# A packed-attention and gated-MLP kernel on one core: its stages rewritten as generators, five conversion adds moved from VectorE to GpSimd, one load of 97 rows made one of 128

## The chip, the cores and the metric

The kernel runs on 1 core of one Trainium2 chip. The metric is the device time of one execution in microseconds (us). The kernel before takes 637.4 us, the median of three runs (636.73 to 638.5).

The engines are named as the profile names them: PE (TensorE's matmuls) and PEld (its weight loads), DVE (VectorE), ACT (ScalarE), POOL (GpSimd), SP (SyncE, which issues every DMA here). Each engine works through its own list of instructions in order.

## What is computed

Three blocks follow each other, for 8 batches of 576 positions and 512 channels.

```
# 1. attention through 32 packed queries per head (8 heads of 64)
p_packed = softmax(p @ k.T / 8) @ v
x = softmax(q @ p_packed.T / 8) @ p_packed
# 2. gated block: causal convolution of 5 taps, w_val and w_out are 512 x 512
gate_pre = sum_k conv_w[k] * xp[:, k:k + S]
x = (sigmoid(gate_pre) * (x @ w_val)) @ w_out
# 3. spatial block: w_in 512 x 1024, w_spatial 576 x 576, w_out2 512 x 512
h = relu(x @ w_in);  u, v = h[..., :512], h[..., 512:]
v_n = (v - mean(v)) / sqrt(var(v) + 1e-6)
v_s = w_spatial @ v_n + b_spatial
out = (u * v_s) @ w_out2
```

The weights of blocks 2 and 3 (except `w_spatial`) arrive as 64-bit floats and are turned into 32-bit ones on the chip.

## The kernel before

**Tiling.** Channels lie on the partitions, in 4 chunks of 128. The 576 positions are taken in two halves of 288, or in row blocks of 128, 128, 128, 128 and 64 (`KT`). Most products are made in three matmuls from a high and a low part of each factor; `split` (L89) makes the parts, the high one with a copy on ACT (L90), the low one with a subtraction on DVE (L91). All products run through `mms` (L93; its matmuls are L95).

**Weights.** `load_raw` (L484) loads 64-bit rows. `from_f64` (L456) turns a 128x512 piece into floats with five instructions in a row: an ACT activation into `tmp` (L460), two integer TENSOR_SCALARs on DVE (L464, L467), one SCALAR_TENSOR_TENSOR on DVE (L468), which writes the destination, and an add (L471), whose engine is an argument, `last`. `unit` (L490) gives `nc.vector` there for the five pieces named in `DADD` (L19) and `nc.gpsimd` for the others. Pieces are `woT` (w_out), `winv` and `winu` (the two halves of w_in) and `wval`; their tokens are `uo`, `uw`, `uu` and `uv`. The temporaries of `uo`, `uw` and `uv` come from four buffers, that of `uu` from one (`late`, L482), so that each `uu` waits for the add of the one ahead.

`fold` (L499, tokens `fv`, `fu`) multiplies w_out by w_in once, so that blocks 2 and 3 share one matrix, `wp`: 4 matmuls of plain 32-bit floats, each of which the profile shows as two instructions, then an ACT copy (L506) and a DVE subtraction (L507).

**Spatial weights.** `spatial` (L509, tokens `ws0` to `ws4`) loads 128 rows of the transposed spatial matrix into a buffer `stage` (L514) and splits them. The fifth, `ws4`, loads the last 64 rows, stored twice, as 128 rows (L517), and then 97 rows more, which hold them again and the bias (L520). From these it makes a copy of 32 rows (L522) and splits rows 0 to 63 and row 96 through a tile `hi` (L90, L91).

**Order of the work.** Three tables list stages by token: `START` (weights, and the first batch's attention), `FIRST` (the first batch's MLP, with the second batch's attention and the rest of the weights in between) and `LOOP` (the same for each further batch, without weights). `run` (L559) calls the stage of each token. The instructions so recorded are then set in order for each engine by a scheduler with a priority in the order of recording; a tile has to find a free buffer of its pool.

**The stages around the change.** `sa` (L136) makes the scores of the packed queries and their exponents, `tr` (L170) transposes them, `av` (L175) multiplies them by v; for the first batch `av` also multiplies by the convolution's taps into `ppk` (L197). `sb` and `sb2` make the second softmax (its normalisation is L239, its transpose L243), `cx` (L283) makes the first batch's gates, `val` (L323) the values times the gates, and `hv` (L349) the normalised rows `vn`: matmuls, a relu on ACT (L364), statistics on DVE (L371 to L375), one power on POOL (L376), and a TENSOR_SCALAR on DVE (L377). The pool `ps2` has four PSUM buffers, which all products share.

Of the kernel before, what the change touches and what calls it, by code (L numbers as in the profile page):

```python
# [16 lines left out]
P = 128  # L17
UGB = 5
DADD = ('u2', 'o0', 'o1', 'w1', 'w0')  # L19
START = """  # L20
ik0 ip0 ro0 ic0 ik1 sa0 iv1 uo0 iv0 rw0 tr0 lv0 rv0 ro1 uo1 cw0 rv1 cb0 lk0 lq0 rw1 uw0 tr1 uo3 uw1 av0 uw2 uo2 uv0 av1 uv1 uw3 lq1 fv3 fv0 fv1 lk1 ppt0 sb0 sb20 sb21 fv2 uv3 uv2 lp0 m0 cx0 cx1 lv1
"""
FIRST = """
val1 ru1 val0 val3 ru0 lv0 val2 sa0 uu2 uu0 hv0 uu1 tr0 ws3 tr1 uu3 fu2 fu0 ws4 hv3 wo0 lv1 ws1 hv2 av0 av1 fu1 lq0 fu3 ppt0 lq1 wo1 hv1 hv4 ws0 sb0 hu1 hu2 ws2 sb20 lp0 hu3 sb21 hu0 wo3 lk0 lk1 sp0 sp2 sp1 wo2 sp3 m0 xt0 out1 xt1 out3 out0 out2
# [7 lines left out]
def packed_attention_gated_mlp(  # L32
# [72 lines left out]
    def load_kq(kind, b, g):  # L105
        src = kT if kind == "k" else qT
        t = kq_p.tile([P, 2, S], F32, tag="kq", name="kq")
        nc.sync.dma_start(out=t, in_=src[b, g])
        kq_t[kind, b, g] = t

    def load_v(b, g):
        t = v_p.tile([P, 4, 5, 65], F32, tag="v", name="v")
        nc.sync.dma_start(out=t, in_=vT[b, g])
        v_t[b, g] = t

    def load_p(b):
        t = sm_p.tile([P, NC * NPK], F32, tag="pbd", name="pbd")
        nc.sync.dma_start(out=t, in_=pT[b])
        pbd_t[b] = t

    class Attn:
        def __init__(self, b):
            self.b = b
            self.a, self.aT = {}, {}
            self.sT, self.A, self.an = {}, {}, {}
            self.gate = {}

# [8 lines left out]
        def sa(self, _):  # L136
            ps, heads = self.heads(pbd_t.pop(self.b), "k")
            for i in range(0, 8, 2):
                for qt in range(4):
                    for g, h, pT_, k in heads[i:i + 2]:  # L140
# [4 lines left out]
                        )  # L145
            mx = sm_p.tile([P, 8], F32, tag="mx", name="mx")
# [13 lines left out]
            for g in range(2):  # L160
                a = f_p.tile([P, S], F32, tag="f", name="a")
# [8 lines left out]
        def tr(self, g):  # L170
            aT = sm_p.tile([P, NB, NPK], F32, tag="aT", name="aT")
            nc.vector.transpose(out=aT.rearrange("p a b -> p (a b)"), in_=self.a.pop(g))
            self.aT[g] = aT

        def av(self, g):  # L175
# [12 lines left out]
            if g == 0:  # L188
# [3 lines left out]
            nc.vector.reciprocal(rs, rs)  # L192
            nc.scalar.activation(out=self.pp[:, g, :], in_=ps[:, :64], func=AF.Copy, scale=rs)
            if self.b == 0:
                if g == 0:
# [6 lines left out]
        def ppt(self, _):  # L202
            ps = ps2.tile([P, 2, 512], F32, tag="ps2", name="ps2")[:, 0, :P]
            nc.tensor.transpose(ps, self.pp.rearrange("p a b -> p (a b)"), ident)
            self.ppT = pp_p.tile([P, P], F32, tag="ppT", name="ppT")
            nc.scalar.copy(out=self.ppT, in_=ps)

        def sb(self, _):
# [8 lines left out]
            for g in range(2):  # L217
                self.softmax_n(g, ps[g])

        def softmax_n(self, g, ps):  # L220
# [8 lines left out]
            )  # L229
            nc.scalar.activation(out=sTf, in_=sTf, func=AF.Exp, scale=scale)  # L230
            self.sT[g] = sT

        def sb2(self, g):
# [9 lines left out]
            nc.vector.transpose(out=an, in_=sT.rearrange("p a b -> p (a b)"))  # L243
            hi = am_p.tile([P, S], F32R, tag="Ah", name="Ah")
            lo = am_p.tile([P, S], F32R, tag="Al", name="Al")
            split(hi, lo, an)
            self.A[g] = (hi, lo)
            self.an[g] = an

        def m(self, _):  # L250
            ps = ps2.tile([P, 2, 512], F32, tag="ps2", name="ps2")
            for h in range(4):
                hs = slice(NPK * h, NPK * h + NPK)
                for g in range(2):
# [4 lines left out]
                    )  # L259
            hi = am_p.tile([P, 2, DM], F32R, tag="Mh", name="Mh", bufs=1)  # L260
            lo = am_p.tile([P, 2, DM], F32R, tag="Ml", name="Ml", bufs=1)
            split(hi, lo, ps)
            self.M = (hi, lo)

        def xt(self, n):
# [9 lines left out]
            if n == 0:  # L275
# [3 lines left out]
            if n == 1:  # L279
                for c in range(4):  # L280
                    self.conv(c, self.x[c // 2][:, c % 2, :])

        def cx(self, n):  # L283
            ps = [ps2.tile([P, 2, 512], F32, tag="ps2", name="ps2") for _ in range(2)]
            for tap in reversed(range(CONV)):
                sft = CONV - 1 - tap
                lo = sft if n == 0 else 0
                for h in range(4):
                    hs = slice(NPK * h, NPK * h + NPK)
                    for g in range(2):  # L290
# [4 lines left out]
                        )  # L295
            for c in range(4):
                if n == 0:
# [5 lines left out]
        def conv(self, c, x):  # L303
            gt = ug_p.tile([P, S], F32, tag="ug", name="gate")
            self.gate[c] = gt
            acc = f_p.tile([P, S], F32, tag="f", name="acc")
            nc.scalar.activation(out=acc, in_=x, func=AF.Copy, scale=cw[:, c, CONV - 1:CONV])  # L307
            for tap in range(CONV - 1):
# [4 lines left out]
                )  # L313
            nc.scalar.activation(out=gt, in_=acc, func=AF.Sigmoid)

    class Mlp:
        def __init__(self, at):
# [3 lines left out]
            self.vn = None  # L321

        def val(self, c):  # L323
# [3 lines left out]
            for n in range(2):  # L327
# [7 lines left out]
                )  # L335
            t = f_p.tile([P, S], F32, tag="f", name="g1")
            nc.vector.tensor_tensor(  # L337
                out=halves(t), in0=ps[:, :, :SH], in1=halves(at.gate.pop(c)), op=ALU.mult
            )
            g = g_p.tile([P, 2, S], F32R, tag="g", name="g")  # L340
            split(g[:, 0, :], g[:, 1, :], t)
            if not self.g1:
# [4 lines left out]
            self.g1[c] = g  # L347

        def hv(self, tt):  # L349
# [11 lines left out]
            vr = vr_p.tile([P, DM], F32, tag="vr", name="vr")  # L361
            if w == P:
                mm3(ps, [((g1[k][:, 0, ts_], g1[k][:, 1, ts_]), (w_hi[k], w_lo[k])) for k in range(NC)])
                nc.scalar.activation(out=vr, in_=ps, func=AF.Relu)  # L364
            else:
                mms(ps, [(self.tail[:, k, :], wk) for k in range(NC) for wk in (w_hi[k], w_lo[k])])
                nc.scalar.copy(out=vr[:w], in_=ps[w:])
                nc.vector.tensor_tensor(out=vr[:w], in0=ps[:w], in1=vr[:w], op=ALU.add)
                nc.scalar.activation(out=vr[:w], in_=vr[:w], func=AF.Relu)
            st = sm_p.tile([P, 6], F32, tag="st", name="st")  # L370
# [16 lines left out]
        def hu(self, c):
            ps = ps2.tile([P, 2, 512], F32, tag="ps2", name="ps2")
            cs = slice(P * c, P * c + P)
            for n in range(2):  # L390
# [10 lines left out]
                )  # L401
            u = ug_p.tile([P, S], F32, tag="ug", name="u")
            nc.scalar.activation(out=halves(u), in_=ps[:, :, :SH], func=AF.Relu)
            self.u[c] = u

        def sp(self, c):
            ps = ps2.tile([P, 2, 512], F32, tag="ps2", name="ps2")
            cs = slice(P * c, P * c + P)
            for n in range(2):
# [12 lines left out]
                )  # L422
            t = f_p.tile([P, S], F32, tag="f", name="g2")
            nc.vector.tensor_tensor(  # L424
                out=halves(t), in0=ps[:, :, :SH], in1=halves(self.u.pop(c)), op=ALU.mult
            )
            g = g_p.tile([P, 2, S], F32R, tag="g", name="g")
            split(g[:, 0, :], g[:, 1, :], t)
            self.g2[c] = g

        def out(self, e):
            ps = ps2.tile([P, 2, 512], F32, tag="ps2", name="ps2")
            cs = slice(P * e, P * e + P)
            for n in range(2):
# [10 lines left out]
                )  # L445
            t = f_p.tile([P, S], F32, tag="f", name="o")
            nc.scalar.copy(out=halves(t), in_=ps[:, :, :SH])  # L447
            nc.sync.dma_start(out=outT[self.b, e], in_=t)
# [7 lines left out]
    def from_f64(dst, raw, n, pool, tag, last=nc.gpsimd):  # L456
# [5 lines left out]
        )  # L462
        ci, ei = c.bitcast(I32), e.bitcast(I32)
# [6 lines left out]
        )  # L470
        last.tensor_tensor(out=dst, in0=dst, in1=c, op=ALU.add)  # L471

    def raw64(slot, srcs):
        n = len(srcs)
        raw = (vn_p if slot == "vn1" else const).tile([P, n, 512, 2], I32, tag=slot, name="raw")
        for i, src in enumerate(srcs):
            nc.sync.dma_start(out=raw[:, i], in_=words(src))
        return [raw[:, i] for i in range(n)]
# [5 lines left out]
    def load_raw(name, slot, w, lo):  # L484
        k0 = int(name[-1]) * 2
        got = raw64(slot, [w[:, k, lo:lo + DM] for k in (k0, k0 + 1)])
        for i in range(2):
            raws[name[:-1], k0 + i] = got[i]

    def unit(kind, k, dst, temps):  # L490
        from_f64(dst, raws.pop((kind, k)), DM, *temps, nc.vector if kind + str(k) in DADD else nc.gpsimd)
# [7 lines left out]
    def fold(m, hf):  # L499
# [4 lines left out]
        mms(ps, [(woT[k][:, cs], win[k]) for k in range(NC)])  # L504
        hi, lo = wp[0][:, m, hs], wp[1][:, m, hs]
        nc.scalar.copy(out=hi, in_=ps)  # L506
        nc.vector.tensor_tensor(out=lo, in0=ps, in1=f32(hi), op=ALU.subtract)  # L507

    def spatial(t):  # L509
        if not ws:  # L510
            ws[:] = [const.tile([P, NT, S], F32R, tag=f"ws{i}", name=f"ws{i}") for i in range(2)]
        st = f_p.tile([P, S], F32, tag="f", name="stage")
        if t < NT - 1:
            nc.sync.dma_start(out=st, in_=wsT[:, t, :])  # L514
            split(ws[0][:, t, :], ws[1][:, t, :], st)
            return
        nc.sync.dma_start(out=st, in_=wsT[:, t, :])  # L517
        nc.scalar.copy(out=ws[0][:, t, :], in_=st)
        st = f_p.tile([P, S], F32, tag="f", name="stage")
        nc.sync.dma_start(out=st[:97], in_=wsT[:97, t + 1, :])  # L520
# [3 lines left out]
        for r in (slice(0, 64), slice(96, 97)):  # L524
            split(hi[r], w[r], st[r])

    def final(k):
        if not wo2:
            wo2[:] = [const.tile([P, NC, DM], F32R, tag=f"wo2{i}", name=f"wo2{i}") for i in range(2)]
        raw = kq_p.tile([P, 512, 2], I32, tag="kq", name="raw")  # L530
        nc.sync.dma_start(out=raw, in_=words(w_out2[:, k, :]))
        t = f_p.tile([P, S], F32, tag="f", name="stage")[:, :DM]
        from_f64(t, raw, DM, *late)
# [140 lines left out]
```

## Time and profile before

| | |
|---|---|
| median of 3 runs | 637.4 us |
| the profiled execution | 639.22 us |
| its span on the core | 637.4 us |
| granted TensorE clock, mean | 0.975 |
| PE busy | 596.7 us (94%) |
| DVE busy | 446.0 us (70%) |
| ACT busy | 292.3 us (46%) |
| POOL busy | 49.3 us (8%) |
| DMA, mean rate | 82 GB/s |

The profiled execution lies 1.8 us outside its span, and the same 1.8 us above the median of the runs. Times of rows are microseconds from the start of the span. START fills the first 70 us, FIRST follows, and then seven passes of LOOP, which start 68.7 us apart. PE is busy 9 tenths of nearly every slice of 16 us from 112 us on; in the first 112 us it is not.

### The profile page before, as it was taken

The page shows a single profiled execution, that of the slowest core. Times are in us where ns is not written, and L with a number is a line of the kernel's source. Part 1 is how long each engine was busy: PE and PEld are TensorE (multiplying, and loading weights), DVE is VectorE, ACT ScalarE, POOL GpSimd, SP SyncE. Part 2 cuts the span into 40 slices and gives each one's busy share as a digit, 9 for nine tenths or more (in the row PEclk, how much of TensorE's full clock was granted, in tenths as well). Part 3 has the DMA queues.
Part 4 walks back from the last instruction along what each step waited for, and adds up shares of the span by engine and source line. Part 5 has one row for each costly group of instructions (what it writes and reads, how often), then busy time and mean ns, then how long its engine had stood idle before and what let it go on. Part 6 is the DMA issues. An engine that isn't in the chain of part 4 may idle for free.

```text
span 637.4 us, 12474 instructions
## 1 busy us (share of the span) xinstructions
PE 596.7 (94%) x5267; PEld 514.7 (81%) x5267; DVE 446.0 (70%) x873; ACT 292.3 (46%) x503; POOL 49.3 (8%) x67
## 2 busy tenths in 40 slices
PE   3687697999999999999999999999999999999997
PEld 2323663898988898899889888989889988989997
DVE  4998355977957696687759685869667875965640
ACT  2522435636463564346543655355533744363422
POOL 1242002200010000100010001000010001000100
PEclk9985797999999999999999999999999999999999
DMA  8960053302322012401222132202240110010001
GB/s 331 408 226 1 1 194 124 127 1 76 114 88 76 20 59 77 159 1 76 80 85 75 53 102 86 75 20 77 64 149 1 75 39 1 2 57 20 1 1 74
DMA packets 16569, 52.48 MB, mean 82 GB/s; under 512 B 1953, under 2 KB 2977, under 8 KB 16514
## 3 DMA queue, kind: packets, MB, share of 16 engines
q1 hardware_dynamic: 16514, 51.70, 22.7%
q8 instruction: 41, 0.67, 0.4%
q14 instruction: 14, 0.11, 0.1%
HBM read 42.25 MB, written 9.44 MB: 81 GB/s over the span
## 4 chain that ended last, share of the span: by engine, by line
PE 80%; DVE 9%; DMA 5%; ACT 3%; POOL 1%; issue 1%; SPq 0%; ACTq 0%; POOLq 0%
PE ps L95 72%; DMA raw<-w_outT 3%; DMA stage<-wsT 2%; PE ps L141 2%; DVE mx L148 2%; PE ps L271 1%; PE ps L181 1%; PE ps L212 1%; ACT L163 1%; DVE tmp L467 1%; PE ps L256 1%; ACT a L163 1%; DVE tmp L464 1%; DVE m L154 1%; POOL winu L471 1%
## 5 line engine op out<-in xcount | busy, mean ns | idle before, releaser
L95 PE MATMUL ps<-ws,vn 128*128 128x288 f32 (+1 forms) x896 | 124.0, 296 | 0.0
L95 PEld LDWEIGHTS ps<-ws,vn 128*128 128x128 f32 (+1 forms) x896 | 120.3, 188 | 2.9 <-issue 2.8
L95 PE MATMUL ps<-g,wp 128*128 128x288 f32 x768 | 113.6, 297 | 0.0
L95 PEld LDWEIGHTS ps<-g,wp 128*128 128x128 f32 x768 | 106.8, 188 | 4.4 <-DVE g L337 1.3
L95 PEld LDWEIGHTS ps<-g,wo 128*128 128x128 f32 x768 | 102.2, 188 | 6.1 <-issue 3.5
L95 PE MATMUL ps<-g,wo 128*128 128x288 f32 x768 | 105.6, 296 | 0.0
L95 PE MATMUL ps<-wp,g 128*128 128x512 f32 x384 | 98.7, 402 | 3.2 <-ACT a L163 3.2
L310 DVE SCALAR_TENSOR_TENSOR acc<-x,cw,acc 128x572 f32<-128x572 f32 (+3 forms) x112 | 82.6, 813 | 24.7 <-ACT acc L307 24.7
L95 PEld LDWEIGHTS ps<-wp,g 128*128 128x128 f32 x384 | 69.6, 188 | 22.1 <-ACT a L163 5.2
L90 ACT CAST g<-g 128x576 fp32r<-128x576 f32 x64 | 43.2, 674 | 73.7 <-DVE g L424 57.1
L376 POOL TENSOR_TENSOR rstd<-rstd,mhalf 128x1 f32<-128x1 f32 (+1 forms) x40 | 24.2, 606 | 460.7 <-DVE rstd L375 460.7
L91 DVE TENSOR_TENSOR g<-g,g 128x576 fp32r<-128x576 f32 x64 | 49.3, 772 | 11.0 <-ACT g L90 10.3
L371 DVE BATCH_NORM_STATS2 st<-vr 128x6 f32<-128x512 f32 (+1 forms) x40 | 27.5, 690 | 30.0 <-ACT vr L364 26.9
L95 PE MATMUL ps<-Ah,Mh 128*128 128x288 f32 x128 | 39.1, 305 | 5.1 <-ACT gate L299 5.1
L90 ACT CAST vn<-vr 128x512 fp32r<-128x512 f32 (+1 forms) x40 | 24.7, 618 | 33.5 <-DVE vr L377 33.5
L95 PE MATMUL ps<-Ah,Ml 128*128 128x288 f32 x128 | 39.0, 305 | 0.0
L95 PE MATMUL ps<-Al,Mh 128*128 128x288 f32 x128 | 39.0, 304 | 0.0
L424 DVE TENSOR_TENSOR g<-ps,u 128x576 f32<-128x576 f32 x32 | 24.1, 754 | 19.1 <-PE ps L95 19.0
L377 DVE TENSOR_SCALAR vr<-vr,mv,rstd 128x512 f32<-128x512 f32 (+1 forms) x40 | 21.5, 538 | 22.5 <-POOL rstd L376 22.4
L447 ACT COPY o<-ps 128x576 f32<-128x576 f32 x32 | 20.3, 635 | 34.8 <-PE ps L95 34.8
L91 DVE TENSOR_TENSOR vn<-vr,vn 128x512 fp32r<-128x512 f32 (+1 forms) x40 | 27.1, 680 | 11.4 <-ACT vn L90 11.3
L364 ACT ACTIVATE vr<-ps 128x512 f32<-128x512 f32 x32 | 19.5, 611 | 30.2 <-PE ps L95 17.4
(111 smaller groups left out, 735.8 us busy)
## 6 DMA issues: line engine op xcount, KB each, us to landing
v<-vT SPq DMA_DIRECT2D x16, 650.0 KB, 5.1
kq<-kT SPq DMA_DIRECT2D x16, 576.0 KB, 4.3
kq<-qT SPq DMA_DIRECT2D x16, 576.0 KB, 4.8
outT<-o SPq DMA_DIRECT2D x32, 288.0 KB, 2.1
raw<-w_in SPq DMA_DIRECT2D x8, 512.0 KB, 10.6
raw<-w_outT SPq DMA_DIRECT2D x4, 512.0 KB, 8.7
raw<-w_val SPq DMA_DIRECT2D x4, 512.0 KB, 9.4
raw<-w_out SPq DMA_DIRECT2D x4, 512.0 KB, 5.2
```

Of the source, the lines that this page charges most:

```text
L90: nc.scalar.copy(out=hi, in_=src)
L91: nc.vector.tensor_tensor(out=lo, in0=src, in1=f32(hi), op=ALU.subtract)
L95: nc.tensor.matmul(out, lhsT=a, rhs=b, start=(i == 0), stop=(i == len(pairs) - 1))
L141: nc.tensor.matmul(ps[g][NPK * qt:NPK * qt + NPK, h // 2, SQ * (h % 2):SQ * (h % 2) + SQ], lhsT=pT_, rhs=k[:, SQ * qt:SQ * qt + SQ], start ...
L148: nc.vector.tensor_reduce(mx[:, 4 * g:4 * g + 4].rearrange("p (a b) -> p a b", a=2), ps[g][:, :, :SH].rearrange("p a (b c) -> p a b c", b= ...
L310: nc.vector.scalar_tensor_tensor(out=acc[:, sft:], in0=x[:, :S - sft], scalar=cw[:, c, tap:tap + 1], in1=acc[:, sft:], op0=ALU.mult, op1=A ...
L364: nc.scalar.activation(out=vr, in_=ps, func=AF.Relu)
L371: nc.vector.bn_stats(st[:w], vr[:w])
L376: nc.gpsimd.tensor_tensor(out=rstd[:w], in0=rstd[:w], in1=mhalf[:w], op=ALU.pow)
L377: nc.vector.tensor_scalar(out=vr[:w], in0=vr[:w], scalar1=mv[:w, 0:1], scalar2=rstd[:w], op0=ALU.subtract, op1=ALU.mult,)
L424: nc.vector.tensor_tensor(out=halves(t), in0=ps[:, :, :SH], in1=halves(self.u.pop(c)), op=ALU.mult)
L447: nc.scalar.copy(out=halves(t), in_=ps[:, :, :SH])
```

## The change

Every stage becomes a generator that yields where the work passes to another engine, and `run` exhausts it; a token may now name a number of steps, which none in the tables does. Tiles are taken just ahead of their first write. The two halves of the second softmax and the four convolutions get tokens of their own, at the place where they ran. `DADD` is empty, so that all conversion adds are on POOL. The second load of `ws4` takes all 128 rows of its block.

```diff
-DADD = ('u2', 'o0', 'o1', 'w1', 'w0')
+DADD = ()
...
-lq0 val1 val0 val2 lp0 val3 hu1 sa0 lq1 hv0 tr0 hv1 hu0 hv4 av0 tr1 av1 hu2 hv2 ppt0 hv3 sb0 sb20 sp1 lv0 sb21 hu3 sp0 sp3 sp2 m0 lk1 xt0 out1 lv1 xt1 out2 out0 lk0 out3
+lq0 val1 val0 val2 lp0 val3 hu1 sa0 lq1 hv0 tr0 hv1 hu0 hv4 av0 tr1 av1 hu2 hv2 ppt0 hv3 sb0 sn0 sn1 sb20 sp1 lv0 sb21 hu3 sp0 sp3 sp2 m0 lk1 xt0 out1 lv1 xt1 cv0 cv1 cv2 cv3 out2 out0 lk0 out3
...
     def split(hi, lo, src):
         nc.scalar.copy(out=hi, in_=src)
+        yield
         nc.vector.tensor_tensor(out=lo, in0=src, in1=f32(hi), op=ALU.subtract)
...
     def spatial(t):
+        st = f_p.tile([P, S], F32, tag="f", name="stage")
+        nc.sync.dma_start(out=st, in_=wsT[:, t, :])
+        yield
         if not ws:
             ws[:] = [const.tile([P, NT, S], F32R, tag=f"ws{i}", name=f"ws{i}") for i in range(2)]
-        st = f_p.tile([P, S], F32, tag="f", name="stage")
         if t < NT - 1:
-            nc.sync.dma_start(out=st, in_=wsT[:, t, :])
-            split(ws[0][:, t, :], ws[1][:, t, :], st)
+            yield from split(ws[0][:, t, :], ws[1][:, t, :], st)
             return
-        nc.sync.dma_start(out=st, in_=wsT[:, t, :])
         nc.scalar.copy(out=ws[0][:, t, :], in_=st)
+        yield
         st = f_p.tile([P, S], F32, tag="f", name="stage")
-        nc.sync.dma_start(out=st[:97], in_=wsT[:97, t + 1, :])
+        nc.sync.dma_start(out=st, in_=wsT[:, t + 1, :])
+        yield
         w = ws[1][:, t, :]
         nc.scalar.copy(out=w[64:96], in_=st[64:96])
         hi = f_p.tile([P, S], F32R, tag="f", name="hi")
         for r in (slice(0, 64), slice(96, 97)):
-            split(hi[r], w[r], st[r])
+            yield from split(hi[r], w[r], st[r])
+            yield
...
+        live = {}
         for tok in order.split():
+            tok, _, n = tok.partition(".")
             name, i = tok[:-1], int(tok[-1])
...
+            for _ in itertools.islice(live[tok] or (), int(n) if n else None):
+                pass
```

**What stands elsewhere on the engines.** On ACT, and in every pass of LOOP on every engine, the rows stand in the same order as before. Three places differ.

The first is in START, on DVE and POOL, where the second piece of `winv` is converted (`ppk` is the attention's result times the convolution's taps, `rs` a reciprocal of a row sum, `tmp` a temporary of the conversion). Before, on DVE:

```order
L468 SCALAR_TENSOR_TENSOR winv<-raw,tmp 128x512
L192 RECIPROCAL rs<-rs 128x1
L471 TENSOR_TENSOR winv<-winv,tmp 128x512
L197 TENSOR_TENSOR ppk<-cwr,pp 128x320
L464 TENSOR_SCALAR tmp<-tmp 128x512
L467 TENSOR_SCALAR tmp<-tmp 128x512
```

Now, on DVE:

```order
L506 SCALAR_TENSOR_TENSOR winv<-raw,tmp 128x512
L202 RECIPROCAL rs<-rs 128x1
L209 TENSOR_TENSOR ppk<-cwr,pp 128x320
L502 TENSOR_SCALAR tmp<-tmp 128x512
L505 TENSOR_SCALAR tmp<-tmp 128x512
```

And on POOL now, from the first add on (`cw` are the taps):

```order
L510 TENSOR_TENSOR woT<-woT,tmp 128x512 x2
L510 TENSOR_TENSOR cw<-cw,tmp 128x20
L510 TENSOR_TENSOR winv<-winv,tmp 128x512
L510 TENSOR_TENSOR woT<-woT,tmp 128x512
L510 TENSOR_TENSOR winv<-winv,tmp 128x512 x2
```

The add of `winv` has left DVE, so that `ppk` stands next there; POOL has two adds of `woT` ahead of `cw`, and two of `winv` that it did not have.

The second is later in START, on DVE, at the first piece of `winu` (`Ml` and `Al` are low parts, `sT` and `an` belong to the second softmax). Before:

```order
L91 TENSOR_TENSOR Ml<-ps_453,Mh 128x1024
L237 TENSOR_SCALAR sm_421<-sm_421 128x18
L91 TENSOR_TENSOR Al<-an,Ah 128x576
L471 TENSOR_TENSOR winu<-winu,tmp 128x512
L238 RECIPROCAL sm_421<-sm_421 128x18
L239 TENSOR_TENSOR sT<-sT,sm_421 128x576
L464 TENSOR_SCALAR tmp<-tmp 128x512
L243 STREAM_TRANSPOSE an<-sT 128x576
L467 TENSOR_SCALAR tmp<-tmp 128x512
L468 SCALAR_TENSOR_TENSOR winu<-raw,tmp 128x512
```

Now:

```order
L93 TENSOR_TENSOR Ml<-ps_453,Mh 128x1024
L252 TENSOR_SCALAR sm_421<-sm_421 128x18
L93 TENSOR_TENSOR Al<-an,Ah 128x576
L253 RECIPROCAL sm_421<-sm_421 128x18
L502 TENSOR_SCALAR tmp<-tmp 128x512
L254 TENSOR_TENSOR sT<-sT,sm_421 128x576
L505 TENSOR_SCALAR tmp<-tmp 128x512
L506 SCALAR_TENSOR_TENSOR winu<-raw,tmp 128x512
L258 STREAM_TRANSPOSE an<-sT 128x576
```

The add has gone to POOL, and the conversion of the next piece stands one step earlier against the softmax.

The third is in FIRST, on SP's queue of loads. Before:

```order
L514 DMA stage<-wsT 128x576
L517 DMA stage<-wsT 128x576
L520 DMA stage<-wsT 97x576
L531 DMA raw<-w_out 128x1024
```

Now:

```order
L549 DMA stage<-wsT 128x576 x2
L559 DMA stage<-wsT 128x576
L549 DMA stage<-wsT 128x576
L570 DMA raw<-w_out 128x1024
```

The load of 97 rows has become one of 128 rows at the same place.

## Rows read from the trace of the kernel before

**Rows 1.** The page: the chain that ended last, by line.

```profile
PE ps L95 72%; DMA raw<-w_outT 3%; DMA stage<-wsT 2%; PE ps L141 2%; DVE mx L148 2%; PE ps L271 1%; PE ps L181 1%; PE ps L212 1%; ACT L163 1%; DVE tmp L467 1%; PE ps L256 1%; ACT a L163 1%; DVE tmp L464 1%; DVE m L154 1%; POOL winu L471 1%
```

**Rows 2.** Chain in order of time, 80 to 160 us (start, us, what).

```profile
83.95 13.35 DMA stage<-wsT
...
97.37 0.68 ACT ws L522
...
101.36 0.61 DVE wp L507
```

**Rows 3.** PE's timeline (start, us, then the instruction; idle before it in brackets).

```profile
79.53 1.24 PE L141 MATMUL ps<-kq,pbd 64*32 64x144 f32 x64
...
82.67 3.60 PE L95 MATMUL ps<-winu,woT 128*128 128x512 f32 x8
...
97.03 0.78 PE L181 MATMUL ps<-v,aT 128*32 128x65 f32 x40
102.02 1.31 PE L181 MATMUL ps<-v,aT 128*32 128x65 f32 x40 [4.21 <-DVE wp L507]
103.26 8.99 PE L95 MATMUL ps<-winu,woT 128*128 128x512 f32 x16
```

**Rows 4.** Stretches: length; busy PE, PEld, DVE, ACT, POOL; clock; DMA share; GB/s.

```profile
93.00:94.00 1.00, 1.00 (x6) 0.82 (x5) 0.00 (x0) 0.00 (x0) 0.00 (x0) 1.00 0.89 316
95.50:97.30 1.80, 1.80 (x25) 1.21 (x27) 0.00 (x0) 0.00 (x0) 0.00 (x0) 1.00 0.07 26
...
100.50:106.50 6.00, 4.48 (x44) 2.58 (x45) 4.58 (x11) 2.96 (x7) 2.06 (x3) 0.50 0.21 44
...
70.00:76.00 6.00, 5.74 (x24) 5.74 (x25) 1.52 (x2) 2.70 (x8) 0.00 (x0) 0.50 0.00 0
```

**Rows 5.** DMA issues between 82 and 92 us (count, KB, us to landing).

```profile
stage<-wsT SPq DMA_DIRECT2D x1, 288.0 KB, 6.1
...
stage<-wsT SPq DMA_DIRECT2D x1, 218.2 KB
...
raw<-w_out SPq DMA_DIRECT2D x1, 512.0 KB, 8.5
stage<-wsT SPq DMA_DIRECT2D x1, 288.0 KB, 8.8
```

**Rows 6.** ACT's timeline around the stall (columns as in rows 3).

```profile
100.45 0.66 ACT L460 ACTIVATE tmp<-raw 128x512 f32<-128x512 f32 x1
...
101.92 0.60 ACT L364 ACTIVATE vr<-ps 128x512 f32<-128x512 f32 x1
```

**Rows 7.** DVE's timeline in START.

```profile
21.89 1.56 DVE L197 TENSOR_TENSOR ppk<-cwr,pp 128x320 f32<-128x320 f32 x1
...
24.49 0.69 DVE L471 TENSOR_TENSOR winv<-winv,tmp 128x512 f32<-128x512 f32 x1
25.09 0.48 DVE L197 TENSOR_TENSOR ppk<-cwr,pp 128x320 f32<-128x320 f32 x1
...
52.51 0.68 DVE L468 SCALAR_TENSOR_TENSOR winu<-raw,tmp 128x512 f32<-128x512 uint32 x1
53.11 1.21 DVE L91 TENSOR_TENSOR Ml<-ps,Mh 128x1024 fp32r<-128x1024 f32 x1
...
54.99 0.68 DVE L471 TENSOR_TENSOR winu<-winu,tmp 128x512 f32<-128x512 f32 x1
```

**Rows 8.** POOL's timeline in START.

```profile
21.72 1.38 POOL L471 TENSOR_TENSOR woT<-woT,tmp 128x512 f32<-128x512 f32 x1 [9.11 <-DVE woT L468]
...
58.70 1.66 POOL L471 TENSOR_TENSOR winu<-winu,tmp 128x512 f32<-128x512 f32 x1 [9.32 <-DVE winu L468]
```

**Rows 9.** Chain in order of time, 0 to 100 us, at the end of START.

```profile
67.53 0.66 ACT tmp L460
...
68.20 1.28 ACT L299
...
70.26 9.35 PE ps L95 x48
```

More of the change, by code (lines that the diff above doesn't have):

```diff
@@ L126, in __init__ @@
             self.gate = {}
+            self.pp = self.ppk = self.x = None
         def heads(self, lhsT, kind):
@@ L216, in sb, with sn @@
                     )
-            for g in range(2):
-                self.softmax_n(g, ps[g])
-        def softmax_n(self, g, ps):
+            self.sps = ps
+            yield
+        def sn(self, g):
+            ps = self.sps[g]
             sT = f_p.tile([P, NB, NPK], F32, tag="f", name="sT")
@@ L278, in xt @@
                 nc.scalar.copy(out=self.x[j][:, :, ss], in_=ps[j][:, :, :SH])
-            if n == 1:
-                for c in range(4):
-                    self.conv(c, self.x[c // 2][:, c % 2, :])
+            yield
         def cx(self, n):
@@ L295, in cx @@
                         )
+            yield
             for c in range(4):
-                if n == 0:
+                if c not in self.gate:
                     self.gate[c] = ug_p.tile([P, S], F32, tag="ug", name="gate")
@@ L313, in conv @@
                 )
+            yield
+            gt = self.gate[c] = ug_p.tile([P, S], F32, tag="ug", name="gate")
             nc.scalar.activation(out=gt, in_=acc, func=AF.Sigmoid)
@@ L339, in val @@
             )
+            yield
             g = g_p.tile([P, 2, S], F32R, tag="g", name="g")
-            split(g[:, 0, :], g[:, 1, :], t)
-            if not self.g1:
+            self.g1[c] = g
+            yield from split(g[:, 0, :], g[:, 1, :], t)
+            if self.tail is None:
                 self.tail = vr_p.tile([P, NC, P], F32R, tag="tail", name="tail", bufs=1)
@@ L426, in sp @@
             )
+            yield
             g = g_p.tile([P, 2, S], F32R, tag="g", name="g")
-            split(g[:, 0, :], g[:, 1, :], t)
             self.g2[c] = g
+            yield from split(g[:, 0, :], g[:, 1, :], t)
         def out(self, e):
@@ L470, in from_f64 @@
         )
+        yield
         last.tensor_tensor(out=dst, in0=dst, in1=c, op=ALU.add)
[L473 to L478, printed above, removed]
     woT, winv, winu = [], [], []
@@ L485, in load_raw @@
         k0 = int(name[-1]) * 2
-        got = raw64(slot, [w[:, k, lo:lo + DM] for k in (k0, k0 + 1)])
+        raw = (vn_p if slot == "vn1" else const).tile([P, 2, 512, 2], I32, tag=slot, name="raw")
         for i in range(2):
-            raws[name[:-1], k0 + i] = got[i]
+            if i:
+                yield
+            nc.sync.dma_start(out=raw[:, i], in_=words(w[:, k0 + i, lo:lo + DM]))
+            raws[name[:-1], k0 + i] = raw[:, i]
     def unit(kind, k, dst, temps):
-        from_f64(dst, raws.pop((kind, k)), DM, *temps, nc.vector if kind + str(k) in DADD else nc.gpsimd)
+        return from_f64(dst, raws.pop((kind, k)), DM, *temps, nc.vector if kind + str(k) in DADD else nc.gpsimd)
     def u_half(k):
@@ L503, in fold @@
         hs = slice(hf * DM, (hf + 1) * DM)
[L504 removed]
+        for k in range(NC):
+            nc.tensor.matmul(ps, lhsT=woT[k][:, cs], rhs=win[k], start=(k == 0), stop=(k == NC - 1))
+            yield
         hi, lo = wp[0][:, m, hs], wp[1][:, m, hs]
         nc.scalar.copy(out=hi, in_=ps)
+        yield
         nc.vector.tensor_tensor(out=lo, in0=ps, in1=f32(hi), op=ALU.subtract)
     def spatial(t):
+        st = f_p.tile([P, S], F32, tag="f", name="stage")
+        nc.sync.dma_start(out=st, in_=wsT[:, t, :])
+        yield
         if not ws:
             ws[:] = [const.tile([P, NT, S], F32R, tag=f"ws{i}", name=f"ws{i}") for i in range(2)]
[L512 to L520 removed]
+        if t < NT - 1:
+            yield from split(ws[0][:, t, :], ws[1][:, t, :], st)
+            return
+        nc.scalar.copy(out=ws[0][:, t, :], in_=st)
+        yield
+        st = f_p.tile([P, S], F32, tag="f", name="stage")
+        nc.sync.dma_start(out=st, in_=wsT[:, t + 1, :])
+        yield
         w = ws[1][:, t, :]
@@ L524, in spatial, with stage @@
         for r in (slice(0, 64), slice(96, 97)):
-            split(hi[r], w[r], st[r])
+            yield from split(hi[r], w[r], st[r])
+            yield
     def final(k):
+        raw = kq_p.tile([P, 512, 2], I32, tag="kq", name="raw")
+        nc.sync.dma_start(out=raw, in_=words(w_out2[:, k, :]))
+        yield
+        t = []
+        def stage():
+            t.append(f_p.tile([P, S], F32, tag="f", name="stage")[:, :DM])
+            return t[0]
+        yield from from_f64(stage, raw, DM, *late)
+        yield
         if not wo2:
             wo2[:] = [const.tile([P, NC, DM], F32R, tag=f"wo2{i}", name=f"wo2{i}") for i in range(2)]
[L530 to L533, printed above, removed]
-        split(wo2[0][:, k, :], wo2[1][:, k, :], t)
+        yield from split(wo2[0][:, k, :], wo2[1][:, k, :], t[0])
     cwr = []
@@ L566, in run @@
             "ru": lambda i: load_raw(f"u{i}", ("ws1", "wo20")[i], w_in, 0),
-            "uo": lambda k: unit("o", k, woT[k], early),
-            "uw": lambda k: unit("w", k, winv[k], early),
-            "uv": lambda k: unit("v", k, wval[:, k, :], early),
-            "uu": lambda k: unit("u", k, u_half(k), late),
+            "uo": lambda k: unit("o", k, lambda: woT[k], early),
+            "uw": lambda k: unit("w", k, lambda: winv[k], early),
+            "uv": lambda k: unit("v", k, lambda: wval[:, k, :], early),
+            "uu": lambda k: unit("u", k, lambda: u_half(k), late),
             "fv": lambda m: fold(m, 1),
@@ L585, in run @@
         }
+        live = {}
         for tok in order.split():
+            tok, _, n = tok.partition(".")
             name, i = tok[:-1], int(tok[-1])
-            if name in setup:
-                setup[name](i)
-            elif name in load:
-                load[name](i)
-            elif hasattr(Mlp, name):
-                getattr(ml, name)(i)
-            elif at:
-                getattr(at, name)(i)
+            if tok not in live:
+                if name in setup:
+                    live[tok] = setup[name](i)
+                elif name in load:
+                    live[tok] = load[name](i)
+                elif hasattr(Mlp, name):
+                    live[tok] = getattr(ml, name)(i)
+                elif at:
+                    live[tok] = getattr(at, name)(i)
+                else:
+                    live[tok] = None
+            for _ in itertools.islice(live[tok] or (), int(n) if n else None):
+                pass
     at = Attn(0)
```

78 lines of the change are left out of this document (56 added, 22 removed).

## The prediction

> **What bounds the kernel now.** I read the page's chain first, then the chain in order of time, then the timelines of PE, ACT, DVE and POOL in the stretches that the change touches. By the page's chain PE's matmuls set 72% of the span [rows 1], and in LOOP the change leaves every engine's list in the same order. So time can come only from the first 112 us. Two lines of that chain that are not PE's lie there: `raw<-w_outT`, 3%, the loads that START begins with, and `stage<-wsT`, 2%.
>
> The second is one transfer. The load of 97 rows is issued at 83.95 us and stands on the chain for 13.35 us, until 97.30 [rows 2]. ACT's cast of it starts at 97.37; behind that, in ACT's fixed order, wait two casts, a cast of `wo` and one of `wp`, and DVE's subtraction for `wp` ends at 101.36 + 0.61 = 101.97 [rows 2]. It frees the PSUM buffer that PE needs for the second `av`: PE's first `av` ends at 97.03 + 0.78 = 97.81, and the second starts at 102.02 after 4.21 us of waiting [rows 3]. The wait costs twice: the granted clock is 0.50 (1.2 GHz) from 100.5 to 106.5 [rows 4], so that this `av` takes 1.31 us where the first took 0.78, and the two folds behind it take 8.99 us, where one took 3.60 at the full clock [rows 3].
>
> The transfer is slow because of its shape. Full loads move at 316 GB/s with a DMA share of 0.89 (93 to 94 us), but from 95.5 to 97.3, just before it lands, the share is 0.07, about one of 16 engines, at 26 GB/s [rows 4]. Its 218.2 KB at 26 GB/s are 8.4 us. Loads of 288 KB with 128 rows, issued within 2 us of it and into the same crowd, landed after 6.1 us [rows 5].
>
> **The change, part by part.** *The load of 128 rows.* It carries 70 KB more, 0.2 us at 316 GB/s, and should land like its neighbours: 6.1 us after issue, at 90.1; at the longest of such loads, 8.8 us, at 92.8 [rows 2, 5]. From landing to the freed buffer the chain now takes 101.97 - 97.30 = 4.67 us. PE wants the buffer at 97.81, so any landing up to 93.1 costs it nothing, and both ends pass. PE then saves the wait, 4.21, on the `av` 1.31 - 0.78 = 0.53, and on the folds 8.99 - 2 x 3.60 = 1.79: together **6.5 us**. What is late next: the first fold needs the buffer that ACT's relu at 101.92 frees; ahead of it in ACT's list is the activation at 100.45, which needs `raw<-w_out` [rows 6]. That load landed 8.5 us after issue, a load of `stage` beside it after 8.8 [rows 5]. They moved with the rest by about 95, when the share fell to one engine [rows 4], and I take their last parts to have stood behind the 97 rows on that engine. Without them ACT is through by some 98, and PE comes to the folds at 98.6. The bounds of this term are 2 us (the rival below) and 6.5. From there on to the end PE is the chain, so what it wins stays won.
>
> *Five adds from DVE to POOL.* An add takes 0.69 us on DVE and 1.38 on POOL [rows 7, 8]. Both pieces of `woT` and the first of `winv` are converted before 20 us, while the chain stands on the loads of `w_outT` [rows 1]; DVE waits for the next piece there, which covers POOL's longer add. I count them 0; without that cover each would cost 0.7. POOL's add of the taps comes up to 1.4 us later behind them, before ACT has finished the exponents that stand ahead of its user; 0.
>
> The second `winv` add is on the path, because it now runs beside `ppk`, a DVE instruction with two inputs in SBUF. The row of the first `ppk` shows the price: it took 1.56 us beside a POOL add that ran from 21.72 to 23.10, and ended at 23.45, 0.35 after it; the second, with POOL idle, took 0.48 [rows 7, 8]. With POOL's add from 24.5 to 25.9 the second would end at 26.25 instead of 25.57: **0.7 us lost**, which DVE, with hardly a gap from there to 53 us, carries on. If it isn't held, nothing.
>
> The `winu` add is a gain. DVE has written the piece at 52.51 + 0.68 = 53.19, but its add waits behind `Ml` and others and ends at 54.99 + 0.68 = 55.67 [rows 7]. POOL can do it by 53.25 + 1.38 = 54.6, 1.0 us earlier. All `uu` pieces share one temporary, so the next activation waits for the add, and this chain of ACT, DVE and POOL runs on to the last activation at 67.53, the gates and `val` at 70.26 [rows 9]. The next add took 1.66 us because a subtraction of DVE had begun ahead of it [rows 8]; with the new order it should take 1.3. Together **1.4 us won**. The unknown is `Ml`, with one input in PSUM and one in SBUF: no POOL add runs beside such an instruction in the trace. If `Ml` held POOL, the add would end at 54.32 + 1.38 = 55.7, as now, and if the subtraction behind it went first too, 0.75 later. I take it as not holding, because the instruction that was held, `ppk`, had both inputs in SBUF. START so gives 1.4 - 0.7 = **0.7 us**, between 1.4 won and 1.4 lost.
>
> The Trainium skill, "SBUF — State Buffer", section "Who interferes with whom", speaks against moving adds to GpSimd: a VectorE instruction with two SBUF inputs waits for the whole of a GpSimd instruction that reads SBUF, as the `ppk` row shows; but one with a single SBUF input does not contend. By that rule `Ml` is harmless and the 1.4 us stand; without it they would be 0 and START would lose 0.7. No row decides it.
>
> *The rest.* Generators, later tiles and new tokens leave order and engines as they were: 0. In FIRST's `sa` five matmuls of each half now stand unpaired; the block takes 1.24 us [rows 3], so 10 of its 32 matmuls could cost 0.4 at most, and DVE is behind there anyway.
>
> **The sum** is 6.5 + 0.7 = 7.2 us. The profiled execution, 639.22 us with a span of 637.4, would become 632.0. It lies 1.8 above the median, so for the median I say 637.4 - 7.2 = **630.2 us**.
>
> **The rivals.** *A clock that doesn't fall.* `val` starts after PE has idled, and from 70 to 76 us the clock is 0.50 [rows 4]; its 48 matmuls take 9.35 us [rows 9]. With `cx` some 1 us later and `val` 0.7 earlier the idle time ahead is shorter. If the clock holds, about 6 us at half speed become 3: 627.2. Against it: a wait of 4.21 us let it fall, and this one would still be about 3. Chance 0.13.
>
> *The next load is the stop.* If `raw<-w_out` still lands 8.5 us after issue, ACT's activation moves from 100.45 only to 99.4, the relu ends near 101.2 instead of 102.5, and the fold starts 2.1 us earlier instead of 4.7, at a fallen clock. 2.1 + 0.7 = 2.8: 634.6. For it: that load is the next in ACT's order. Against: the DMA engines were nearly idle when it was due. Chance 0.13.
>
> *The load does not do what its shape says*, and lands late all the same: then only START is left, 637.4 - 0.7 = 636.7, no change that can be told. Loads of the same shape beside it speak against that. Chance 0.05.
>
> *POOL becomes the gate: slower.* Each moved add takes 0.7 us longer and can hold one DVE instruction for 1.56 - 0.48 = 1.08. If all five lay on START's chain, it would lose 5 x 1.78 = 8.9 us, more than FIRST wins: 637.4 - 6.5 + 8.9 = 639.8. It decides against the change from 1.7 us an add. Three of the five stand where DVE waits for loads, and one shortens a wait. Chance 0.04.
>
> **How the numbers follow.** My forecast has 0.65. Its own range is START's two ends, 629.5 to 632.3. The range for 8 in 10 reaches down to the clock rival and up towards the late load: 627.2 to 634.0. A run can tell a change of 0.3%, 1.9 us, from none. Forecast, clock and late load are all faster by more: 0.65 + 0.13 + 0.13 = 0.91; the same 0.05; slower 0.04.
>
> **What would show it.** Right: the chain no longer holds `stage<-wsT`; that load lands some 6 us after issue; PE has no wait of 4 us between its two `av`; the folds take about 7.2 us at the full clock; `ppk` twice takes over 1 us; `val` starts near 69.5; LOOP's passes still take 68.7 us. Wrong: a wait of ACT for `raw<-w_out` of about 3 us, adds on POOL with DVE waiting behind each, or another pitch of the passes.

## The result and the profile after

The changed kernel takes 630.79 us, the median of four runs (629.62 to 631.95), beside 637.95 for the kernel before (four runs, 636.73 to 639.11). The ratio is 0.9888 with a 95% interval of 0.9857 to 0.9919: 7.1 us faster, between 5.2 and 9.1. The forecast was 7.2. That the two meet within 0.1 us is luck: the interval is 4 us wide, and a second set, below, gives 8.6 us. The two profiled executions lie further apart, spans of 637.4 and 627.8 us, 9.6 in all; why, is told below.

The page's chain of the changed kernel, by line:

```profile
PE ps L97 73%; DMA raw<-w_outT 3%; PE ps L540 2%; PE ps L147 2%; DVE mx L155 2%; PE ps L288 1%; PE ps L190 1%; ACT L171 1%; PE ps L225 1%; DVE tmp L505 1%; PE ps L272 1%; ACT a L171 1%; DVE nb L166 1%; DVE m L161 1%; DVE tmp L502 1%
```

The load of `stage`, 2% before [rows 1], has left the chain. PE's folds stand there on a line of their own (L540) only because they are written apart from `mms` now. LOOP's passes start 68.7 us apart, as before.

PE's timeline of the changed kernel (start, us, the instruction, idle time before it in brackets), at `val`, the folds and the two `av`:

```profile
68.61 0.40 PE L97 MATMUL ps<-Ah,Mh 128*128 128x288 f32 x1 [3.17 <-ACT gate L316]
...
76.70 1.41 PE L147 MATMUL ps<-kq,pbd 64*32 64x144 f32 x64
...
80.02 3.60 PE L540 MATMUL ps<-winu,woT 128*128 128x512 f32 x8
...
94.20 1.36 PE L190 MATMUL ps<-v,aT 128*32 128x65 f32 x80
95.49 7.13 PE L540 MATMUL ps<-winu,woT 128*128 128x512 f32 x16
```

Compare [rows 3]. The two `av` now run as one row of 1.36 us with no wait between them, and the two folds take 7.13 us instead of 8.99. From the first `av` to the end of the folds it was 97.03 to 112.25, 15.22 us; now it is 94.20 to 102.62, 8.42: 6.8 us less.

DMA issues around that place (count, KB each, median us to landing). First a line of the kernel before that stands with [rows 5]: the load of `stage` with 128 rows that was issued at 84.30 us, right behind the 97 rows:

```profile
stage<-wsT SPq DMA_DIRECT2D x1, 288.0 KB, 13.7
```

Then the changed kernel, three loads of `stage` first, the new load of 128 rows (issued at 80.63), the one ahead of it and the one behind it (81.07):

```profile
stage<-wsT SPq DMA_DIRECT2D x3, 288.0 KB, 5.7
...
raw<-w_out SPq DMA_DIRECT2D x1, 512.0 KB, 4.2
stage<-wsT SPq DMA_DIRECT2D x1, 288.0 KB, 4.5
```

The loads issued behind it gained as well: the one right behind it lands after 6.0 us where it took 13.7; `raw<-w_out` lands after 4.2 us where it took 8.5, the `stage` load beside it after 4.5 where it took 8.8 [rows 5].

POOL's timeline of the changed kernel at the two adds that matter, then DVE's at the same places:

```profile
23.98 1.27 POOL L510 TENSOR_TENSOR winv<-winv,tmp 128x512 f32<-128x512 f32 x1 [1.43 <-DVE rs L202]
...
53.30 1.27 POOL L510 TENSOR_TENSOR winu<-winu,tmp 128x512 f32<-128x512 f32 x1 [3.94 <-DVE winu L506]
57.42 1.27 POOL L510 TENSOR_TENSOR winu<-winu,tmp 128x512 f32<-128x512 f32 x1 [2.85 <-DVE winu L506]
```

```profile
24.42 1.18 DVE L209 TENSOR_TENSOR ppk<-cwr,pp 128x320 f32<-128x320 f32 x1 [0.44 <-ACT pp L204]
...
52.49 0.68 DVE L506 SCALAR_TENSOR_TENSOR winu<-raw,tmp 128x512 f32<-128x512 uint32 x1
53.09 1.21 DVE L93 TENSOR_TENSOR Ml<-ps,Mh 128x1024 fp32r<-128x1024 f32 x1
54.23 0.37 DVE L252 TENSOR_SCALAR sm<-sm 128x18 f32<-128x18 f32 x1
```

The second `ppk` is held: 1.18 us instead of 0.48 [rows 7], until 25.60, 0.35 after POOL's add. `Ml` is not: 1.21 us as before, with POOL's add beside it from 53.30, which isn't lengthened either. The next add of `winu` takes 1.27 us, like that one, instead of 1.66 [rows 8]. From the start of the first `winu` piece's SCALAR_TENSOR_TENSOR to `val` it was 52.51 to 70.26, 17.75 us [rows 7, 9]; now it is 52.49 to 68.61, 16.12: 1.6 us less.

### The profile page after: what moved, and what is told of

It is laid out like the page before. It is cut to its first block, busy times and chain, and to the rows that moved or that the text cites. A ratio compares the mean times of both kernels' runs of the same rounds, so it can differ in the third digit from the quotient of the medians.

```text
span 627.8 us, 12477 instructions
## 1 busy us (share of the span) xinstructions
PE 593.3 (95%) x5267; PEld 512.4 (82%) x5267; DVE 445.5 (71%) x868; ACT 292.2 (47%) x503; POOL 53.7 (9%) x72
## 4 chain that ended last, share of the span: by engine, by line
PE 82%; DVE 9%; ACT 3%; DMA 3%; issue 1%; POOL 1%; SPq 0%; ACTq 0%; POOLq 0%
PE ps L97 73%; DMA raw<-w_outT 3%; PE ps L540 2%; PE ps L147 2%; DVE mx L155 2%; PE ps L288 1%; PE ps L190 1%; ACT L171 1%; PE ps L225 1%; DVE tmp L505 1%; PE ps L272 1%; ACT a L171 1%; DVE nb L166 1%; DVE m L161 1%; DVE tmp L502 1%
## 6 DMA issues: line engine op xcount, KB each, us to landing
raw<-w_val SPq DMA_DIRECT2D x4, 512.0 KB, 10.2
```

## The experiments

Theory: the 97 rows held ACT, ACT held DVE, and DVE the buffer that PE wanted; the `winu` add on POOL shortens START; the `winv` add there costs a hold of `ppk`. Rivals: the load was hidden and the gain is another part's; POOL's adds cost; the later tiles do it; a load of fewer than 128 rows is slow as such.

### The load alone

```diff
 # the kernel before
-        nc.sync.dma_start(out=st[:97], in_=wsT[:97, t + 1, :])
+        nc.sync.dma_start(out=st, in_=wsT[:, t + 1, :])
```

> The kernel before with one edit: the second load of ws4 takes 128 rows. Theory (the load's shape holds ACT and through it PE): 6.5 to 6.8 us faster than before, no wait of PE between its two av, the load lands about 6 us after issue, START as before with val at about 70.3. Rival (the gain comes with the adds or the rewriting, the load being hidden): less than 2 us faster.

Measured: 634.04 us (six runs) beside 639.25 for the kernel before (20 runs, which also serve the adds alone, the rewriting alone and the first set on `ppk`); ratio 0.9909, 0.9891 to 0.9928: 5.8 us faster, between 4.6 and 7.0. PE's timeline:

```profile
71.62 0.61 PE L95 MATMUL ps<-Ah,Mh 128*128 128x288 f32 x1 [6.16 <-ACT gate L299]
...
97.38 1.36 PE L181 MATMUL ps<-v,aT 128*32 128x65 f32 x80
98.66 7.13 PE L95 MATMUL ps<-winu,woT 128*128 128x512 f32 x16
```

The wait is gone with this edit alone, the folds are at the full clock, and no load of `stage` takes longer than 6.1 us. `val` starts at 71.6, not at 70.3: the granted clock was 0.72 from 37 to 43 us, where the profile before has 1.00, and the first `winu` piece came 1.4 later (53.87); more on that clock below. This is most of the gain. Its median lies under the 6.5 to 6.8 expected, its interval holds them.

### The adds alone

```diff
 # the kernel before
-DADD = ('u2', 'o0', 'o1', 'w1', 'w0')
+DADD = ()
```

> The kernel before with one edit: all conversion adds on POOL, the load still 97 rows. Theory: 0.7 to 1.6 us faster (the winu add about 1.6 earlier, the second ppk about 0.5 later), val near 69.2, the wait of PE for the load still there, though started earlier. Rival (POOL holds DVE so often that the adds cost): 0 to 3 us slower.

Measured: 637.31 us (nine runs); ratio 0.9968, 0.9951 to 0.9984: 2.0 us faster, between 1.0 and 3.1. DVE's timeline, and then PE's:

```profile
24.86 1.19 DVE L197 TENSOR_TENSOR ppk<-cwr,pp 128x320 f32<-128x320 f32 x1 [0.44 <-ACT pp L193]
...
55.34 0.68 DVE L468 SCALAR_TENSOR_TENSOR winu<-raw,tmp 128x512 f32<-128x512 uint32 x1
```

```profile
71.45 0.61 PE L95 MATMUL ps<-Ah,Mh 128*128 128x288 f32 x1 [3.67 <-ACT gate L299]
...
102.61 1.31 PE L181 MATMUL ps<-v,aT 128*32 128x65 f32 x40 [4.80 <-DVE wp L507]
```

`ppk` is held; from the `winu` piece to `val` it is 71.45 - 55.34 = 16.11 us, as in the changed kernel, and the wait for the 97 rows is back. The adds are a gain, so the rival that they cost falls. Against the forecast `val` is 2 us late, because the `winu` piece came at 55.3 instead of 52.5; the clock was 0.52 from 37 to 43 us here.

### The rewriting alone

```diff
 # the changed kernel
-DADD = ()
+DADD = ('u2', 'o0', 'o1', 'w1', 'w0')
...
-        nc.sync.dma_start(out=st, in_=wsT[:, t + 1, :])
+        nc.sync.dma_start(out=st[:97], in_=wsT[:97, t + 1, :])
```

> The changed kernel with both of its visible edits undone: the five adds back on DVE, 97 rows. What is left is generators, later tiles and new tokens. Theory: the same as before within 1 us, every stretch of the profile alike. Rival (later tiles free buffers for loads and win part of the time): 1 to 3 us faster.

Measured: 639.02 us (twelve runs); ratio 0.9997, 0.9982 to 1.0012. Generators, later tiles and new tokens change nothing that can be told; the profile has PE's wait between the two `av` again, 4.65 us, though not every stretch alike, since the clock from 37 to 43 us was 0.72 here. The load's 5.8 and the adds' 2.0 make 7.8 us, inside the interval of the whole change.

### Which numbers of rows are slow

```diff
 # the changed kernel, n = 101, 112, 100
-        nc.sync.dma_start(out=st, in_=wsT[:, t + 1, :])
+        nc.sync.dma_start(out=st[:n], in_=wsT[:n, t + 1, :])
```

> The changed kernel with 101 rows in the second load of ws4 (a prime number again). Theory (the number of rows decides over how many DMA engines a load is spread, and a prime goes to one): it lands 12 to 15 us after issue at a DMA share near 0.07, PE waits some 4 us, about 636.5 us. Rival (97 rows were slow because a load of fewer than 128 rows, or one that ends inside a group of rows, is): the same slowness here, but then also with 112 and 100 rows.

> The changed kernel with 112 rows in the second load of ws4 (7 times 16). Theory (spread by divisors): it lands as the 128 rows do, about 6 us after issue, PE does not wait. Rival (any load of fewer than 128 rows is slow): 12 to 15 us.

> The changed kernel with 100 rows (10 times 10). Theory (spread by divisors, so over 10 engines): it lands 6 to 7 us after issue, PE does not wait. Rival (any load of fewer than 128 rows, or one whose rows do not fill 16 engines, is slow): 12 to 15 us, as with 97.

Measured, one execution each: 639.62 us with 101 rows, 631.98 with 112, 629.70 with 100; the kernel before has 638.96 (11 runs) beside the first and 638.39 (one run) beside the other two. With 101 rows, the chain in order of time (start, us, what), a stretch just before the load lands (columns as in [rows 4]), and the landing times of the loads of `stage`. The view has no landing for the load of 101 rows, nor for the one of 100 below; the 14.8 us are the load of 128 rows right behind the 101:

```profile
83.64 14.42 DMA stage<-wsT
```

```profile
96.00:98.00 2.00, 1.91 (x46) 1.24 (x44) 0.00 (x0) 0.00 (x0) 0.00 (x0) 1.00 0.07 25
```

```profile
DMA to landing us min/median/max: 5.6/7.6/14.8
```

The same line with 112 rows, then with 100, and there ACT's copy of what the 100 rows brought (its start, 87.9 us, stands behind its length in ns):

```profile
DMA to landing us min/median/max: 4.4/6.2/6.6
```

```profile
DMA to landing us min/median/max: 4.4/6.1/7.2
L562 ACT CAST ws<-stage x1: 667/667/667, 87.9 to 87.9; 32x576 fp32r<-32x576 f32 x1
```

With 101 rows the load again takes 14.4 us, in the end at a share of 0.07, about one engine of 16, and PE waits 4.88 us between its two `av`. With 112 rows it lands after 6.5 us; the 100 rows, issued at 80.8, have landed when ACT's copy starts at 87.9, some 7 us after; and the wait is gone in both. So neither "fewer than 128 rows" nor "few rows in the last group" is what is slow. The time with 101 rows came out 3 us above what was expected; both places of the clock told of below were low in that execution, 0.72 from 37 to 43 us and 0.57 from 69 to 77.

The Trainium skill, "DMA: Bandwidth & Descriptors", section "Why a DMA increments its semaphore by 16 and not by 1", gives the rule: a load runs on the largest number of engines, up to 16, that divides its number of rows, and so on 1 for a prime, on 16 for 112 or 128, on 10 for 100. The runs agree for 97 and 101 (share 0.07), and for 112 and 128 as far as these land like their neighbours; that it was ten engines with 100 rows no row here shows.

### The hold of `ppk`, and one execution against another

```diff
 # the changed kernel, for w1_again; after_again has no edit
-DADD = ()
+DADD = ('w1',)
```

> The changed kernel with the second winv add alone back on DVE. Theory (that add on POOL holds ppk): 0.5 us faster than the changed kernel, the second ppk back from 1.18 to about 0.5 us. Rival (DVE's add of 0.69 costs as much as the hold of 0.7): no difference, the steps after it at the same times.

> The changed kernel unaltered, on one chip with the next two. It should again be 6.5 to 8 us faster than before. The profile tells what differs from one execution of a kernel to another: by the clock theory, only the places in START and at val where the clock falls; by its rival (loads that land at other times), the first activations of the conversion.

> The changed kernel with the second winv add back on DVE, beside the changed kernel itself. Theory (the hold of ppk alone): 0.5 us faster. Theory with the clock (PE idles less ahead of val, so that the clock falls later or not at all there): 0.5 us and in some executions 1.5 more, 1 to 2 us in the median. Rival: no difference.

Measured: in the first set 629.61 us (four runs), ratio to before 0.9852 (0.9831 to 0.9872). In the second set, side by side, with 638.96 for the kernel before (11 runs), the changed kernel took 630.10 (six runs; ratio 0.9866, 0.9841 to 0.9890: 8.6 us faster, between 7.0 and 10.2) and the one with the add back 630.07 (six runs; 0.9864, 0.9840 to 0.9889): no difference, so that the 1 to 2 us of the theory with the clock did not come. DVE's rows of `ppk` in that set, the changed kernel first:

```profile
24.56 1.19 DVE L209 TENSOR_TENSOR ppk<-cwr,pp 128x320 f32<-128x320 f32 x1 [0.44 <-ACT pp L204]
```

```profile
25.04 0.48 DVE L209 TENSOR_TENSOR ppk<-cwr,pp 128x320 f32<-128x320 f32 x1
```

The hold goes, as expected, but DVE gets its add of 0.69 us back. By rows a hold costs about 0.5: in the kernel before, from the start of the add to the end of `ppk`, it was 24.49 to 25.57, 1.08 us [rows 7]; in the changed kernel 23.98 to 25.60, 1.62. DVE does carry it on: from the SCALAR_TENSOR_TENSOR of that `winv` piece to that of the first `winu` piece it is 28.74 us in the kernel before, 28.73 with the add back (second set) and 29.26 in the changed kernel, in three executions with a clock of 1.00 from 37 to 43 us. Half a microsecond is less than the times of whole runs can tell, since executions of the changed kernel in this set lie up to 2.9 us apart.

What sets them apart is seen in two executions of the same changed kernel, its first profile and this one, of 627.8 and 630.4 us. Stretches of the first (columns as in [rows 4]):

```profile
37.00:43.00 6.00, 5.22 (x25) 2.14 (x26) 5.12 (x9) 3.37 (x6) 2.29 (x4) 1.00 0.33 121
69.00:77.00 8.00, 8.00 (x68) 7.83 (x74) 4.02 (x7) 3.40 (x8) 0.00 (x0) 0.79 0.00 0
```

and of the second:

```profile
37.00:43.00 6.00, 5.09 (x18) 1.99 (x22) 3.91 (x7) 2.26 (x5) 2.42 (x4) 0.72 0.27 108
69.00:77.00 8.00, 6.97 (x32) 6.97 (x33) 2.32 (x4) 3.47 (x11) 0.00 (x0) 0.57 0.00 0
```

In the second the granted clock falls to 1.2 GHz once more, among START's folds from 37 us on (0.72 instead of 1.00), and longer at `val` (0.57 instead of 0.79). The first goes with 1.3 us: the `winu` piece starts at 53.92 instead of 52.49, of which 0.13 was there at 23 us already. The second goes with 1.1: from the start of `val` to the start of the first fold of `winu` it is 70.03 to 82.58, 12.55 us, instead of 68.61 to 80.02, 11.41. Together 2.4 of the 2.6 us between the two spans. By these rows it is the clock, and loads that land at other times can account for the 0.13 at most.

### A version that beats both

```diff
 # the changed kernel
-DADD = ()
+DADD = ('w1', 'u0', 'u1', 'u3')
```

> The changed kernel with the second winv add and the adds of winu 0, 1 and 3 on DVE; winu 2 stays on POOL. Theory (each add of that chain on POOL is 0.6 us longer, and val waits for the chain): the adds of winu 1 and 3 save 0.6 us each and ppk 0.5, so 1.8 us faster than the changed kernel, up to 3 where the clock no longer falls ahead of val. Rival (something else holds val, as the end of cx or the gates): at most 0.5 us.

Measured: 628.03 us (five runs); ratio to before 0.9830 (0.9806 to 0.9853), 10.9 us faster, between 9.4 and 12.4, and 2.1 less in the median than the changed kernel beside it; all five runs lie below its six (626.58 to 629.30, 629.47 to 632.32). PE's row at `val`, and DVE's at the two adds that were to gain:

```profile
66.92 0.40 PE L97 MATMUL ps<-Ah,Mh 128*128 128x288 f32 x1 [2.45 <-ACT gate L316]
```

```profile
60.51 0.69 DVE L510 TENSOR_TENSOR winu<-winu,tmp 128x512 f32<-128x512 f32 x1
...
63.46 0.69 DVE L510 TENSOR_TENSOR winu<-winu,tmp 128x512 f32<-128x512 f32 x1
```

From the first `winu` piece, at 52.05 here, to `val` it is 14.87 us instead of 16.12: 1.25 us, twice the 0.6 by which an add is shorter on DVE; the `winv` add back on DVE gives the 0.5 of above. In this chain an add is best on the engine that is free when its piece is ready: POOL for `winu` 2, when DVE has a queue, and DVE for 1 and 3, when it waits. `u0` is even: from its piece's SCALAR_TENSOR_TENSOR to that of the next piece it is 3.58 us, and 3.59 with its add on POOL.

## Why the prediction was right

**The load.** Forecast 6.5 us, by the sum of the wait, the second `av` and the folds. The profiled pair shows 6.8 for that stretch, the load alone 5.8 (4.6 to 7.0). The rows of the kernel before already held the answer: a share of one engine before the landing, and equal loads ahead of it that took less than half as long (6.1 and 5.8 us). One reading was wrong on the way: 8.8 us was not the longest of the loads of 128 rows. The one right behind the 97 rows took 13.7 (line above), which [rows 5] leave out; a landing that late would have missed the margin, and it speaks for the rival of a load that stays slow. The mechanism of the prediction covers it, since that load too was behind the 97 rows and lands after 6.1 us with the load alone changed, but the prediction did not say so. The margin was read rightly too: the load had to land by 93.1, in a stretch that ran 2.8 us later than now; issued at 80.63 it lands at about 86.3, some 4 us before the margin, so that its exact time did not matter. That the 97 rows made the next load in ACT's order late was argued there and is now shown: 4.2 us instead of 8.5, and 4.1 with the load alone changed. That it stood on the same DMA engine fits the rows of before, a share of 0.06 at 25 GB/s from 97.3 to 98.3, when the 97 rows have landed and the loads behind them have not; which engine it was no row shows. ACT still waits 1.69 us for that load, off PE's path.

**The adds.** Forecast 0.7 us, as 1.4 won at `winu` and 0.7 lost at `ppk`. The rows say 1.6 and 0.5, so 1.1; the runs of the adds alone say 2.0 (1.0 to 3.1), so that 0.7 was too little. Both terms had their sign and place right and were mis-sized by 0.2. The first add ends 1.1 us earlier and the next is 0.4 shorter, within 0.1 of the forecast; the 0.2 lie between them (from the end of one to the start of the other 2.85 us instead of 3.03), where DVE's conversion now stands one step earlier. The second was too large because POOL's add took 1.27 us there and not 1.38. In the times of the profiled pair `ppk`'s loss is hidden: the activation that START's chain waits for began at 18.90 us instead of 19.44. What the runs have above the rows' 1.1 may be the clock at `val`; that is not shown.

`Ml` was the open price. It came out as forecast, but the reason given, that only an instruction with two SBUF inputs had been held, was not what the trace of before shows. A TENSOR_SCALAR of the conversion, with one, was held beside POOL's add of 27.10 to 28.49, where it otherwise takes 0.43:

```profile
27.40 1.38 DVE L467 TENSOR_SCALAR tmp<-tmp 128x512 int32<-128x512 int32 x1
```

The Trainium skill's rule ("SBUF — State Buffer", section "Who interferes with whom") has a condition that the prediction left out: a VectorE instruction with at most one SBUF input does not contend unless it runs in a two-port mode, and the page counts TENSOR_SCALAR, not TENSOR_TENSOR, among those that can. The trace agrees on both: 1.38 for this row, 1.21 for `Ml` and 1.27 for the add beside it.

**What was counted at nothing.** The three early adds, which no run moved by themselves, cost nothing in the rows: from the SCALAR_TENSOR_TENSOR of the first `winv` piece to the row sum behind it is 2.81 us before (17.10 to 19.91) and now (16.48 to 19.29), and that piece starts no later. The rewriting alone measures 0.9997. The unpaired matmuls of `sa` cost 0.17 us (1.41 instead of 1.24 [rows 3]), and PE waits 0.17 less behind them.

**The rivals.** The one of the clock came true in part in the first profiled execution: PE's idle time before `val` fell from 5.05 us to 3.17, the clock still fell, but for half as long, and `val`'s 48 matmuls took 8.18 us instead of 9.35 [rows 9]. That is 1.2 us that the forecast did not have. In the second it is 9.25 us from `val`'s start to the next row of PE, as before (9.27). In the profile of the version with the `winv` add back, first set, the clock stayed at 1.00 from 69 to 77 us. The late next load, the load that stays slow, and POOL as the gate are refuted by the rows above.

**The 9.6 us of the two profiles against the 7.1 of the runs.** 1.6 of START, 1.2 of the clock at `val` and 6.8 of the load make 9.6. The execution profiled before was 1.3 us above the median of its runs and the one after 1.2 below; without these 2.5 the two agree.

## What to carry to other kernels

When a load is late, look at the DMA share just before it lands: 0.07 is about one engine of 16, and then the number of rows is worth changing, here 97 to 128 at the price of 70 KB. The loads issued behind it are late with it, so their times are no measure of what such a load takes. A transfer that an engine waits for in order also holds everything behind it on that engine, so its price is read at the engine that is short of work at the end of that chain, clock included, and the margin up to which it may be late is worth working out. Moving small work to a second engine paid here where the first had a queue at that moment (`winu` 2), and cost where it hadn't (`winu` 1 and 3) or where the moved add held the first engine's next instruction (`ppk`); decide it for each instruction.

## What the runs showed of the hardware that was not expected

One slow load delays the loads behind it, though these have 128 rows: one issued 0.35 us later took 13.7 us and 6.1 with the load alone changed; two issued 7 us later landed 4.3 us later than in the changed kernel. It holds SP too: the issue of the load right behind it took SP 2.19 us with 97 rows and 4.26 with 101, but 0.42 with the load alone changed.

The granted clock falls at different places from one execution of the same program to the next, and in the pair compared above that is most of the difference: 2.4 of 2.6 us. How long PE idles ahead of `val` does not decide it alone: with 2.50 us of idle time the clock held there (the run with 100 rows), with 2.45 it fell (the version that beats both). What decides was not tried.

A DVE instruction of 18 columns, the TENSOR_SCALAR on `sm`, was held too: 0.37 us beside POOL's `winu` add, 0.16 in the kernel before. And three TENSOR_SCALARs like the one shown above, 1.37 to 1.38 us instead of 0.43, stand on START's chain in both kernels (at 27.4, 29.7 and 32.1 us). Each loses some 0.95 to an add on POOL that would take 0.69 on DVE; by that estimate these adds would be 0.26 better on DVE, which was not tried.
